# Moving the gate and up loads, and the work that needs them, in front of wq and K in a single-token decode kernel

## Chip, cores, metric

One core of one Trainium2 chip. The metric is the device time of one execution in microseconds (us), as a median of several. A kernel's executions mostly spread over 2 to 3 us. An execution counts as slow when it is over 1.5% above the fastest of the same kernel.

The engines go by short names: PE (TensorE, the matrix products; PEld its weight loads), DVE (VectorE), ACT (ScalarE), POOL (GpSimd) and SP (SyncE, which issues the loads; SPq is its queue of instructions). HBM is the memory that holds the inputs, SBUF the on-chip memory that the engines read. PE's granted clock is the share of its full clock that it was given.

## The reference

One token passes through attention over a long cache and through a feed-forward network, and a sigmoid gate mixes the two:

```python
# x: [1,1,512]; K, V: [1,32,65536,128]; wq: [512,4096]; wo: [4096,512]
# w_gate, w_up: [512,1792]; w_down: [1792,512]; all bf16
q = (x @ wq).reshape(32 heads, 128)
p = softmax(q . K * 128**-0.5)            # per head, over 65536 positions
a = (p @ V).reshape(4096) @ wo
b = (silu(x @ w_gate) * (x @ w_up)) @ w_down
g = sigmoid((x * gate_w).sum())
out = g * a + (1 - g) * b
```

K and V are 1073.7 MB together. Everything else is about 14 MB. Each byte is used once.

## The kernel before

SBUF holds a ring of three buffers ("slots") of 64 KB per partition. The work goes in 64 steps of 8.4 MB of K and 8.4 MB of V each (K0, V0, K1, V1, ...). A step multiplies K by q on DVE, in place, sums the products on PE against an identity, takes the exponential, and multiplies with V on PE ("P·V"). A load into a slot is issued on the SP queue and waits there until the slot's last reader has finished (K1's waited 47.0 us for the last gate/up product). In the first turn, wq, gate and up share the slot that K1 takes later:

```python
WQ = KT * H * Dh
wq_sb = view(0, 0, KT, H * Dh)
dma("wq", wq_sb, A_wq.rearrange("(p t) f -> p t f", t=KT), units(0, 0, WQ))
dma("x", x_row, A_x[0], ["x_row"], engine="ACT")
dma("gw", gw_row, gate_w.unsqueeze(0), ["gw_row"], engine="ACT")
# ... load(): each K or V step goes to the next of the three slots
load("k", 0, [EK] * (KPP // EK))          # four pieces of 64 rows per partition
G0, U0 = WQ, WQ + KT * F
gate_v, up_v = view(0, G0, KT, F), view(0, U0, KT, F)
dma("gate", gate_v, ...); dma("up", up_v, ...)
load("v", 0, [KPP])
# ... the q products: 128 matmuls of one column, reading wq
spread(0)
for n in range(N - 1):
    if n:
        load("k", n, [KPP]); load("v", n, [KPP])
    m = HK if n else EK
    for j in range(0, KPP, m):
        block(n, j, m)                    # K times q on DVE, sums on PE
        # ... elif n == N - 2: norm(0, H - 1); outputs()
        # ... gather(): reduce the sums on DVE, exp on ACT
    gather()
    if n == 0:
        gate()                            # the mixing gate
        hidden()                          # 112 gate/up matmuls, silu, product
    pv(n)
# the last step: w_down, wo, K63 in four pieces, V63 in five,
# with the down product and the attention output between the score blocks
```

The softmax here doesn't subtract the row's maximum and nothing guards it: scores larger than these inputs give would overflow.

## Time and profile before

| | before |
|---|---|
| time, median | 2522.44 us of 3 runs (2521.55 to 2523.16) |
| span of the profiled run | 2520.2 us |
| bytes moved, mean rate | 1088 MB, 432 GB/s |
| DMA, PE, DVE busy | 99.7%, 79%, 50% of the span |

These are lines of the page of the kernel before: span, busy time of each engine, the rate in 40 slices of 63 us, and the DMA queue that carries the loads.

```profile
span 2520.2 us, 19415 instructions
...
PE 1979.0 (79%) x9115; PEld 823.1 (33%) x9115; DVE 1268.4 (50%) x286; ACT 97.4 (4%) x398; POOL 1.9 (0%) x9
...
GB/s 423 430 432 433 435 433 434 434 435 436 435 435 434 433 434 435 434 434 434 435 436 434 435 433 434 434 435 435 434 433 435 436 435 435 433 433 434 436 429 359
...
q1 hardware_dynamic: 20880, 1087.78, 99.7%
```

The loads fill the span. Only the first slice (423) and the last two (429, 359) fall below the rate of the rest.

The windows view gives busy time per stretch; its last three columns are PE's granted clock, the DMA share and the rate. This is the kernel before, with its heading and two stretches of it:

```profile
core 0: us, PE busy (x) PEld busy (x) DVE busy (x) ACT busy (x) POOL busy (x), PEclk, DMA share, GB/s
...
55.00:60.00 5.00, 0.00 (x0) 0.00 (x0) 0.00 (x0) 0.00 (x0) 0.00 (x0) 0.50 1.03 446
...
80.00:2469.00 2389.00, 1888.81 (x8153) 772.70 (x8153) 1224.58 (x251) 90.04 (x369) 0.00 (x0) 0.91 1.00 434
```

In 2389 us in the middle the DMA share is 1.00 at 434 GB/s.

The third view is the DMA queue's own timeline in the opening (start, duration of the issue, what is loaded):

```profile
1.02 0.37 SPq L179 DMA_DIRECT2D slot_65<-in_A_wq_dram  x1
1.44 1.98 SPq L179 DMA_DIRECT2D slot_66<-in_A_k_cache_dram  x4
3.46 0.47 SPq L179 DMA_DIRECT2D slot_65<-in_B_w_gate_dram  x1
3.97 0.49 SPq L179 DMA_DIRECT2D slot_65<-in_B_w_up_dram  x1
4.50 0.45 SPq L179 DMA_DIRECT2D slot_67<-in_A_v_cache_dram  x1
51.96 0.33 SPq L179 DMA_DIRECT2D slot_65<-in_A_k_cache_dram  x1
52.33 0.43 SPq L179 DMA_DIRECT2D slot_66<-in_A_v_cache_dram  x1
77.94 0.33 SPq L179 DMA_DIRECT2D slot_67<-in_A_k_cache_dram  x1
```

The first eight loads are issued in the first 5 us and stand in the queue (V0 landed 57.4 us after its issue). K1 (slot_65) follows at 51.96 us, when the last gate/up product has ended. V1 (slot_66) stands behind it in the queue's order.

PE waited for two loads in the first 63 us. The first line is its wait for wq (us in total, times, longest); the second is P·V of step 0 from the timeline (start, duration, instruction, and in brackets how long PE was idle before it and what it waited for, here V0):

```profile
PE m_x L265 <- DMA slot_65<-in_A_wq_dram: 10.8, 1, 10.8
...
61.93 15.98 PE L251 MATMUL O_ps<-slot_67,P_sb_83 128*4 128x512 bf16 x64 [10.01 <-DMA slot_67<-in_A_v_cache_dram]
```

### The profile page before, as it was taken

Reading aid. Unit: us, or ns where it says so; the run is one execution under the profiler, and the core shown is the slowest. Engines: PE = TensorE matmul, PEld = TensorE weight load, DVE = VectorE, ACT = ScalarE, POOL = GpSimd, SP = SyncE. Lnnn points to the kernel's source line nnn. Section 1 sums busy time; section 2 is a strip of 40 time slices with the busy share of each in tenths; the row PEclk is TensorE's granted clock in tenths of the full one; section 3 lists DMA queues with packets and bytes.
Section 4 is the critical chain, followed back from the end, with each engine's and each line's share of the span. In section 5 each row is a group of like instructions: output and inputs, shape, how many; then the busy total and the mean of one; then the engine's idle time right before and its main releaser. Section 6 shows DMA issues by size and latency. Waiting matters only on the chain.

```text
span 2520.2 us, 19415 instructions
## 1 busy us (share of the span) xinstructions
PE 1979.0 (79%) x9115; PEld 823.1 (33%) x9115; DVE 1268.4 (50%) x286; ACT 97.4 (4%) x398; POOL 1.9 (0%) x9
## 2 busy tenths in 40 slices
PE   4787877877778778778787787787787877877878
PEld 2233332333333333333333333333333332333334
DVE  3455355464553554644645546446455455464553
ACT  0000000000000000000000000000000000000000
POOL 0000000000000000000000000000000000000000
PEclk8888988989889899899898898998998988989888
DMA  9999999999999999999999999999999999999998
GB/s 423 430 432 433 435 433 434 434 435 436 435 435 434 433 434 435 434 434 434 435 436 434 435 433 434 434 435 435 434 433 435 436 435 435 433 433 434 436 429 359
DMA packets 20906, 1088.09 MB, mean 432 GB/s; under 512 B 2450, under 2 KB 2580, under 8 KB 2836
## 3 DMA queue, kind: packets, MB, share of 16 engines
q1 hardware_dynamic: 20880, 1087.78, 99.7%
q8 instruction: 16, 0.26, 0.0%
q14 instruction: 6, 0.05, 0.0%
q10 hardware_dynamic: 4, 0.00, 0.0%
HBM read 1087.77 MB, written 0.00 MB: 432 GB/s over the span
## 4 chain that ended last, share of the span: by engine, by line
DMA 44%; PE 41%; DVE 13%; ACT 1%; another core or an unknown queue 0%; issue 0%; SPq 0%; DVEq 0%; ACTq 0%
PE O_ps L251 18%; DMA slot_67<-in_A_k_cache_dram 16%; DMA slot_66<-in_A_k_cache_dram 14%; DMA slot_65<-in_A_k_cache_dram 14%; PE S_ps_101 L265 12%; PE S_ps_102 L265 9%; DVE slot_66 L324 4%; DVE slot_67 L324 4%; DVE slot_65 L324 3%; DVE S_sb_82 L349 2%; PE m_c L251 2%; PE m_x L265 1%; ACT P_sb_83 L274 1%; DMA slot_65<-in_A_wq_dram 0%
## 5 line engine op out<-in xcount | busy, mean ns | idle before, releaser
L265 PE MATMUL S_ps_101<-slot_67,ident 128*128 128x512 bf16 x704 | 204.1, 462 | 134.5 <-DVE slot_67 L324 134.5
L265 PE MATMUL S_ps_101<-slot_66,ident 128*128 128x512 bf16 x672 | 196.6, 464 | 128.3 <-DVE slot_66 L324 128.3
L265 PE MATMUL S_ps_101<-slot_65,ident 128*128 128x512 bf16 x672 | 189.6, 452 | 132.6 <-DVE slot_65 L324 132.6
L324 DVE TENSOR_TENSOR slot_67<-slot_67,q_bc_79 128x16384 bf16<-128x16384 bf16 (+1 forms) x26 | 207.9, 8033 | 142.0 <-DMA slot_67<-in_A_k_cache_dram 142.0
L349 DVE TENSOR_REDUCE S_sb_82<-S_ps_102 128x128 f32<-128x1024 f32 (+1 forms) x66 | 78.7, 1192 | 387.9 <-PE S_ps_102 L265 387.9
L324 DVE TENSOR_TENSOR slot_65<-slot_65,q_bc_78 128x16384 bf16<-128x16384 bf16 x22 | 190.2, 8689 | 145.7 <-DMA slot_65<-in_A_k_cache_dram 145.7
L324 DVE TENSOR_TENSOR slot_66<-slot_66,q_bc_78 128x16384 bf16<-128x16384 bf16 (+1 forms) x24 | 190.6, 7977 | 136.1 <-DMA slot_66<-in_A_k_cache_dram 120.4
L324 DVE TENSOR_TENSOR slot_67<-slot_67,q_bc_78 128x16384 bf16<-128x16384 bf16 x20 | 172.9, 8689 | 121.9 <-DMA slot_67<-in_A_k_cache_dram 121.9
L324 DVE TENSOR_TENSOR slot_66<-slot_66,q_bc_79 128x16384 bf16<-128x16384 bf16 x20 | 172.9, 8688 | 118.7 <-DMA slot_66<-in_A_k_cache_dram 118.7
L324 DVE TENSOR_TENSOR slot_65<-slot_65,q_bc_79 128x16384 bf16<-128x16384 bf16 x20 | 172.9, 8689 | 118.5 <-DMA slot_65<-in_A_k_cache_dram 118.5
L251 PE MATMUL O_ps<-slot_67,P_sb_83 128*4 128x512 bf16 x704 | 155.7, 382 | 28.3 <-ACT P_sb_83 L274 18.3
L251 PE MATMUL O_ps<-slot_65,P_sb_83 128*4 128x512 bf16 x704 | 155.2, 381 | 20.7 <-ACT P_sb_83 L274 20.7
L251 PE MATMUL O_ps<-slot_66,P_sb_84 128*4 128x512 bf16 x704 | 153.7, 379 | 19.3 <-ACT P_sb_84 L274 19.3
L265 PEld LDWEIGHTS S_ps_101<-slot_67,ident 128*128 128x128 bf16 x704 | 79.1, 115 | 258.9 <-DVE slot_67 L324 145.1
L265 PEld LDWEIGHTS S_ps_101<-slot_66,ident 128*128 128x128 bf16 x672 | 75.7, 116 | 249.1 <-DVE slot_66 L324 139.0
L265 PE MATMUL S_ps_102<-slot_67,ident 128*128 128x512 bf16 x704 | 155.9, 379 | 0.2 <-DVE slot_67 L324 0.2
L265 PEld LDWEIGHTS S_ps_101<-slot_65,ident 128*128 128x128 bf16 x672 | 74.1, 113 | 248.4 <-DVE slot_65 L324 143.2
L251 PE MATMUL O_ps<-slot_65,P_sb_84 128*4 128x512 bf16 x640 | 139.7, 379 | 18.3 <-ACT P_sb_84 L274 18.3
L251 PE MATMUL O_ps<-slot_67,P_sb_84 128*4 128x512 bf16 x640 | 139.7, 379 | 18.3 <-ACT P_sb_84 L274 18.3
L251 PE MATMUL O_ps<-slot_66,P_sb_83 128*4 128x512 bf16 x640 | 139.7, 379 | 17.5 <-ACT P_sb_83 L274 17.5
L265 PE MATMUL S_ps_102<-slot_66,ident 128*128 128x512 bf16 x672 | 148.7, 379 | 1.3 <-DVE slot_66 L324 1.3
L265 PE MATMUL S_ps_102<-slot_65,ident 128*128 128x512 bf16 x672 | 148.6, 379 | 0.1
(83 smaller groups left out, 860.1 us busy)
## 6 DMA issues: line engine op xcount, KB each, us to landing
slot_66<-in_A_k_cache_dram SPq DMA_DIRECT2D x4, 2048.0 KB, 24.7
slot_67<-in_A_k_cache_dram SPq DMA_DIRECT2D x4, 2048.0 KB, 23.9
slot_65<-in_A_wq_dram SPq DMA_DIRECT2D x1, 4096.0 KB, 12.3
slot_66<-in_A_wo_dram SPq DMA_DIRECT2D x1, 4096.0 KB, 30.7
slot_65<-in_A_v_cache_dram SPq DMA_DIRECT2D x1, 4096.0 KB, 17.6
slot_65<-in_A_v_cache_dram SPq DMA_DIRECT2D x1, 2048.0 KB, 22.1
slot_65<-in_B_w_gate_dram SPq DMA_DIRECT2D x1, 1792.0 KB, 34.9
slot_65<-in_B_w_up_dram SPq DMA_DIRECT2D x1, 1792.0 KB, 38.6
```

Of the source, the lines that this page charges most:

```text
L251: ins = nc.tensor.matmul(out_ap, lhsT=a, rhs=b, start=start and i == 0, stop=stop and i == len(pairs) - 1,)
L265: ins = nc.tensor.matmul(out_ap, lhsT=a, rhs=b, start=(i == 0), stop=(i == len(pairs) - 1))
L274: "ACT", key, lambda: nc.scalar.activation(out=out_ap, in_=in_ap, func=func, **kw),
L324: "products", lambda: nc.vector.tensor_tensor(out=w, in0=w, in1=q_rep, op=ALU.mult),
L349: lambda: nc.vector.tensor_reduce(out=S_sb[b][:, :m], in_=S_ps[r][:, :m, :], axis=AXIS.X, op=ALU.add),
```

## The change

Its intent is to put the gate/up products and the mixing gate into the time in which PE waits for wq, so that they no longer stand between the scores of step 0 and its P·V. For that gate and up are loaded first, then wq, then K0. No byte and no matmul is added or removed. The diff, complete:

```diff
--- before.py
+++ after.py
@@ -183,6 +183,10 @@
 
     WQ = KT * H * Dh
     wq_sb = view(0, 0, KT, H * Dh)
+    G0, U0 = WQ, WQ + KT * F
+    gate_v, up_v = view(0, G0, KT, F), view(0, U0, KT, F)
+    dma("gate", gate_v, B_w_gate.rearrange("(p t) f -> p t f", t=KT), units(0, G0, U0))
+    dma("up", up_v, B_w_up.rearrange("(p t) f -> p t f", t=KT), units(0, U0, U0 + KT * F))
     dma("wq", wq_sb, A_wq.rearrange("(p t) f -> p t f", t=KT), units(0, 0, WQ))
     dma("x", x_row, A_x[0], ["x_row"], engine="ACT")
     dma("gw", gw_row, gate_w.unsqueeze(0), ["gw_row"], engine="ACT")
@@ -214,10 +218,6 @@
         assert at == KPP
 
     load("k", 0, [EK] * (KPP // EK))
-    G0, U0 = WQ, WQ + KT * F
-    gate_v, up_v = view(0, G0, KT, F), view(0, U0, KT, F)
-    dma("gate", gate_v, B_w_gate.rearrange("(p t) f -> p t f", t=KT), units(0, G0, U0))
-    dma("up", up_v, B_w_up.rearrange("(p t) f -> p t f", t=KT), units(0, U0, U0 + KT * F))
     load("v", 0, [KPP])
 
 
@@ -288,20 +288,6 @@
         ["x_row", "ones_b"], ["m_x"],
     )
     dve("Xc", lambda: nc.vector.tensor_copy(out=Xc, in_=m_x[:, :KT]), ["m_x"], ["Xc"])
-
-
-    group(
-        "q_ps",
-        [
-            (
-                m_x[:, h : h + 1],
-                [(wq_sb[:, t, h * Dh : (h + 1) * Dh], Xc[:, t : t + 1]) for t in range(KT)],
-            )
-            for h in range(H)
-        ],
-        units(0, 0, WQ) + ["Xc"], ["m_x"],
-    )
-    act("qT", qT, m_x[:, :H], ACT.Copy, ["m_x"], ["qT"])
 
     def spread(h):
 
@@ -497,6 +483,21 @@
 
     V_END = [KPP // 2, KPP // 4, KPP // 8, KPP // 16, KPP // 16]
     cut = {}
+    gate()
+    hidden()
+
+    group(
+        "q_ps",
+        [
+            (
+                m_x[:, h : h + 1],
+                [(wq_sb[:, t, h * Dh : (h + 1) * Dh], Xc[:, t : t + 1]) for t in range(KT)],
+            )
+            for h in range(H)
+        ],
+        units(0, 0, WQ) + ["Xc"], ["m_x"],
+    )
+    act("qT", qT, m_x[:, :H], ACT.Copy, ["m_x"], ["qT"])
     spread(0)
     for n in range(N - 1):
         h, c = divmod(n, CH)
@@ -519,9 +520,6 @@
             while len(todo) > 1:
                 gather()
         gather()
-        if n == 0:
-            gate()
-            hidden()
         if n == N - 2:
             turn_outputs(0)
         pv(n)
```

## The prediction

> # Prediction
>
> **What bounds the kernel now.** The DMA engines. The page gives the hardware queue 99.7% of 16 engines' span and a mean of 432 GB/s; 1087.8 MB at the 434 GB/s of most slices is about 2506 us of a 2520 us span (an estimate from those numbers). PE is busy 79% (1979 us), DVE 50% (1268 us). [...]
>
> **The opening, where the change is.** In windows of 5 us, the DMA share is 0.63 in the first and 0.95 or more in every one to 100 us: the queue never runs dry. The DMA-queue timeline shows why: later loads are issued ahead of their turn. K of step 1 (into the buffer of wq, gate and up) is issued at 51.96 us, after the last gate/up product, while V of step 0 lands until 61.93 us (PE's wait for it ends there): 10 us to spare. V of step 1 is issued at 52.33 us, behind it.
>
> **What the change does.** No byte and no matmul is added or removed: the same loads go out in another order, and the 112 gate/up matmuls (6.85 us), the mixing gate (about 2 us) and six small ACT/DVE steps (about 1.4 us) move from after K0's scores to the wait for wq. PE idles there now: 10.8 us until 13.38 us.
>
> Estimates from this trace's rate and landings:
> - gate+up (3.67 MB) take 8.5 us and land near 12 us; their products end at 16 to 19 us; wq lands near 22 us instead of 13.4; the 128 q matmuls (3.58 us) end near 25.5 us.
> - DVE's first K product starts near 27 us instead of 18.46. The K pieces land every 4.8 us, the last near 41 us; scores are ready near 50 us instead of 44.
> - V0 lands at 62 us as before, since the same bytes precede it. P·V of step 0 starts there in both kernels: the 8.5 us lost on K are absorbed by PE's wait for V0 (10 us now, about 11 then, since gate/up no longer stand in it).
> - K1 is issued near 25.5 us instead of 52 and only sits in the queue longer; V1 near 49.5 us instead of 52.3, held by K0's last sums.
>
> **On the critical path: about 0 us.** From 62 us on both kernels should be in the same state, and the end is untouched (last DMA bytes at about 2511 us, then the last products and the output). What remains is noise of the tail: PE runs without a gap from 2469 to 2511 us, and its granted clock there (0.69 to 1.00 in windows) can move the end by a microsecond or two.
>
> **Predicted time:** 2522.4 us, range 2519.0 to 2526.0. Chances: faster by over 2% 0.005, within 2% 0.99, slower 0.005.
>
> **What would show it right.** DMA share near 1 from 5 us on; gate/up matmuls at 12 to 19 us, q matmuls at 22 us, first K product at 27 us; K1 issued at 25 us; P·V of step 0 starting within 1 us of 62 us; GB/s from the second slice on unchanged.
>
> **What would make it wrong.** If DMA really starved between 45 and 62 us, an earlier K1 would gain up to a few us. If the shorter runs per partition of gate and up (14 KB against 32 KB of wq) slow the first transfers, that costs directly. If K now paces the scores past 62 us, V1's issue slips, but it would have to slip past about 80 us to cost anything. Another phase of PE's clock in the last 50 us could move the time 1 to 2 us for no reason in the change.

The 2522.4 us are the time of the kernel before (2522.44 us) with about 0 us on the critical path.

## More of the kernel before

The gate/up matmuls read their weights at a step of 14 columns, so that hidden unit `p*14+ft` falls on partition p, as w_down is laid out:

```python
[(wv[:, t, bass.ds(ft, P, FT)], Xc[:, t : t + 1]) for t in range(KT)]
```

## The result, and the profile after

The changed kernel took 2521.99 us (median of 4 runs, 2521.67 to 2523.99), the kernel before 2522.29 us (4 runs). The ratio is 1.000, with a 95% interval of 0.9983 to 1.0018: the same time. A ratio here is the mean time of one kernel's fast runs over that of the other's of the same rounds, so it is not quite the ratio of the medians.

The same lines of the page of the changed kernel:

```profile
span 2520.0 us, 19416 instructions
...
PE 1979.7 (79%) x9115; PEld 823.9 (33%) x9115; DVE 1268.3 (50%) x286; ACT 97.4 (4%) x398; POOL 1.9 (0%) x9
...
q1 hardware_dynamic: 20880, 1087.78, 99.7%
```

The window of the middle (same columns as before):

```profile
80.00:2469.00 2389.00, 1889.01 (x8153) 773.23 (x8153) 1224.45 (x251) 90.06 (x368) 0.00 (x0) 0.91 1.00 434
```

Busy times, bytes and rate are unchanged.

The queue's timeline after the change:

```profile
1.03 0.37 SPq L179 DMA_DIRECT2D slot_65<-in_B_w_gate_dram  x1
1.45 0.43 SPq L179 DMA_DIRECT2D slot_65<-in_B_w_up_dram  x1
1.92 0.42 SPq L179 DMA_DIRECT2D slot_65<-in_A_wq_dram  x1
2.39 2.35 SPq L179 DMA_DIRECT2D slot_66<-in_A_k_cache_dram  x4
4.79 0.45 SPq L179 DMA_DIRECT2D slot_67<-in_A_v_cache_dram  x1
26.92 0.33 SPq L179 DMA_DIRECT2D slot_65<-in_A_k_cache_dram  x1
53.14 0.33 SPq L179 DMA_DIRECT2D slot_66<-in_A_v_cache_dram  x1
78.04 0.33 SPq L179 DMA_DIRECT2D slot_67<-in_A_k_cache_dram  x1
```

K1 is now issued at 26.92 us, 25 us earlier. V1 is issued at 53.14 us, K2 (slot_67) at 78.04 us against 77.94 us: the advance is gone when the ring has turned once, because K2 needs V0's slot, and V0 lands when it did before. PE's waits, and P·V of step 0, show the same thing:

```profile
PE m_x L265 <- DMA slot_65<-in_B_w_up_dram: 5.4, 1, 5.4
...
PE m_x L265 <- DMA slot_65<-in_A_wq_dram: 3.4, 1, 3.4
...
62.01 16.01 PE L251 MATMUL O_ps<-slot_67,P_sb_83 128*4 128x512 bf16 x64 [8.90 <-DMA slot_67<-in_A_v_cache_dram]
```

PE's wait for V0 ended at 61.93 us before and ends at 62.01 us now. The wait for wq went from 10.8 to 3.4 us, and a wait of 5.4 us for up was added. The work did move into the idle time as intended. The end of the idle time did not move, since the same bytes come before V0 in any order.

### The profile page after: what moved, and what is told of

Same layout as the page of the kernel before. It is cut to its first block, busy times and chain, and to the rows that moved or that the text cites. A ratio compares the mean times of both kernels' runs of the same rounds, so it can differ in the third digit from the quotient of the medians.

```text
span 2520.0 us, 19416 instructions
## 1 busy us (share of the span) xinstructions
PE 1979.7 (79%) x9115; PEld 823.9 (33%) x9115; DVE 1268.3 (50%) x286; ACT 97.4 (4%) x398; POOL 1.9 (0%) x9
## 3 DMA queue, kind: packets, MB, share of 16 engines
q1 hardware_dynamic: 20880, 1087.78, 99.7%
## 4 chain that ended last, share of the span: by engine, by line
DMA 45%; PE 41%; DVE 13%; ACT 1%; issue 0%; another core or an unknown queue 0%; SPq 0%; DVEq 0%; ACTq 0%
PE O_ps L251 18%; DMA slot_67<-in_A_k_cache_dram 16%; DMA slot_66<-in_A_k_cache_dram 14%; DMA slot_65<-in_A_k_cache_dram 14%; PE S_ps_101 L265 12%; PE S_ps_102 L265 9%; DVE slot_66 L310 4%; DVE slot_67 L310 4%; DVE slot_65 L310 3%; DVE S_sb_82 L335 2%; PE m_c L251 2%; DMA slot_65<-in_A_wq_dram 1%; ACT P_sb_83 L274 1%; PE m_x L265 0%
## 5 line engine op out<-in xcount | busy, mean ns | idle before, releaser
L251 PE MATMUL O_ps<-slot_66,P_sb_84 128*4 128x512 bf16 x704 | 153.7, 379 | 19.3 <-ACT P_sb_84 L274 19.3
```

The lines of the kernel that those rows point to most:

```text
L251: ins = nc.tensor.matmul(out_ap, lhsT=a, rhs=b, start=start and i == 0, stop=stop and i == len(pairs) - 1,)
```

## Experiments

The theory to be tested (Q): the DMA queue sets the time; what PE and DVE do in the opening costs nothing as long as the next load is issued before the queue runs dry. The rival (C): the opening's work is on the critical path, and the change made two real shifts that cancel, about 9 us gained by clearing the way from scores to P·V and about 9 us lost by loading K0 later. Both fit a ratio of 1.000. Twelve kernels were run. They were timed in batches. Each batch ran on one chip, with runs of the kernel before among them, and a kernel is compared only with those of its own batch (the factors 2 and 6 below were in another batch, on another chip, than the factor 4).

Medians against the kernel before of the same rounds ("K62 ready" is the start of DVE's first product on the K of step 62 in the profiled run, 2439.53 us in the kernel before):

| run | this, us (runs) | before, us (runs) | ratio, 95% interval | K62 ready, us |
|---|---|---|---|---|
| loads_only | 2526.41 (5) | 2522.78 (9) | 1.0013, 1.0000 to 1.0027 | 2442.64 |
| pe_only | 2523.78 (5) | 2522.78 (9) | 1.0004, 0.9990 to 1.0017 | 2441.56 |
| before_gu2 | 2523.57 (5) | 2522.98 (9) | 1.0001, 0.9987 to 1.0015 | 2440.52 |
| before_gu4 | 2535.54 (4) | 2522.78 (9) | 1.0050, 1.0034 to 1.0065 | 2451.98 |
| after_gu4 | 2524.25 (4) | 2522.78 (9) | 1.0005, 0.9990 to 1.0020 | 2440.01 |
| after_gu6 | 2527.00 (4) | 2522.98 (9) | 1.0017, 1.0002 to 1.0032 | 2444.21 |
| no_up | 2518.07 (5) | 2522.98 (9) | 0.9981, 0.9967 to 0.9994 | 2435.24 |
| down_early | 2525.21 (5) | 2522.98 (9) | 1.0010, 0.9996 to 1.0023 | 2443.98 |
| tail_pieces | 2522.43 (5) | 2522.41 (9) | 0.9999, 0.9985 to 1.0012 | in pieces |
| tail_pieces_down | 2522.28 (5) | 2522.41 (9) | 1.0000, 0.9986 to 1.0013 | in pieces |
| tail_pieces_before | 2521.29 (5) | 2522.41 (9) | 0.9997, 0.9984 to 1.0011 | in pieces |
| gu_contig | 2522.03 (1, state unknown) | 2524.17 (1, state unknown) | none | |

The intervals are about 0.0013 (3 us) wide on each side. Where a time differs by less, the trace's own instants are what is read.

Not every time fell into the range expected. Those of before_gu4, after_gu6 and no_up did. Those of pe_only, before_gu2 and after_gu4 lie up to 0.6 us above the range that Q gave, and that of loads_only 1.4 us; down_early and the three tail_pieces kernels missed theirs too. Each of these was slower than expected, none faster.

### The two halves of the change, each alone

loads_only takes the new order of loads and leaves PE's order as it was:

```diff
 wq_sb = view(0, 0, KT, H * Dh)
+dma("gate", ...); dma("up", ...)
 dma("wq", ...)
 ...
 load("k", 0, ...)
-dma("gate", ...); dma("up", ...)
```

> The new load order with the old order on PE (gate/up products after the scores of K0). Theory Q (the DMA queue sets the time; work in the opening is free as long as the next load is issued before the queue runs dry): K0's scores end near 54 us as in the changed kernel, the gate/up products run from about 55 to 62 us, so K1 is issued at about 62 us, at the very moment when V0's last bytes land: the queue runs dry for 1 to 2 us and the time is 2523 to 2525 us. Rival C (the opening's work is on the critical path; the change gains about 9 us by clearing the work between K0's scores and P*V of step 0, and loses about 9 us by loading K0 later): this half has the loss alone, so about 2531 us.

Measured: 3.6 us slower (2526.41 against 2522.78 us; no run of the one overlaps the other's).

```profile
60.91 0.33 SPq L179 DMA_DIRECT2D slot<-in_A_k_cache_dram  x1
...
84.22 17.29 DVE L324 TENSOR_TENSOR slot<-slot,q_bc 128x16384 bf16<-128x16384 bf16 x2 [21.96 <-DMA slot<-in_A_k_cache_dram]
```

K1 was issued at 60.91 us, and the first product on K1 started at 84.22 us, 3.0 us later than the 81.20 us of the kernel before. K62 was ready 3.1 us late. That is more than the dry time of 1 to 2 us expected, although K1 was issued a little earlier than foreseen (the margin was mis-sized, see the points below), and far less than the 9 us of C.

pe_only does the reverse: PE's new order (gate/up, then q), and the loads in the old order. Its edit is against the changed kernel:

```diff
-dma("gate", ...); dma("up", ...)        # in front of wq
 dma("wq", ...)
 ...
 load("k", 0, ...)
+dma("gate", ...); dma("up", ...)
```

> The old load order with the new order on PE (gate/up products before the q products, so q waits for up, which lands last). Q: gate/up products 42.6 to 49.5 us, q until 53 us, K1 issued near 53 us (before V0 has landed at 62 us), first K product near 54.5 us instead of 18.5, K0's scores near 80 us, P*V of step 0 at 80 us instead of 62, V1 issued near 79 us, just before K1's bytes end at about 81: time 2522 to 2523.5 us although the first step is 18 us late. C: 15 to 20 us slower, about 2540 us.

These are lines of its timeline (start, duration, instruction):

```profile
54.99 8.76 DVE L310 TENSOR_TENSOR slot<-slot,q_bc 128x8192 bf16<-128x8192 bf16 x2 [5.46 <-ACT q_bc L274]
...
79.25 0.33 SPq L179 DMA_DIRECT2D slot<-in_A_v_cache_dram  x1
...
80.38 13.97 PE L251 MATMUL O_ps<-slot,P_sb 128*4 128x512 bf16 x64 [1.16 <-ACT P_sb L274]
```

DVE's first product comes at 54.99 us instead of 18.46 us, and P·V of step 0 begins at 80.38 us, 18 us late. The time is 2523.78 us, 1.0 us above the kernel before and inside the noise of the timing. C's 15 to 20 us are not there. What is there is small and visible in the trace: K62 was ready 2.0 us late. K1, issued at 53.52 us, was in time (its first product at 81.16 us, against 81.20 us in the kernel before). V1, issued at 79.25 us, was not, so by Q it found the queue run dry. The window from 79 to 80 us shows no bytes (0 GB/s), but one empty microsecond proves little: the kernel before has one too, from 58 to 59 us, with K1 long in its queue.

So neither half gives the gain or the loss that C needs; C falls.

### How much slack there was: gate/up products made two, four or six times

The edit is one factor, in either kernel; the result stays right, since each pass overwrites the last:

```diff
-group("gu", parts, ...)
+group("gu", parts * 4, ...)             # 2, 4 or 6
```

> The kernel before with the gate/up products made twice. Q: K1 is issued at 51.96 + 6.85 = 58.8 us, 2 to 3 us before V0's bytes end: within the margin, so 2522 to 2523 us. Rival C: plus 6.85 us, 2529 us.

> The kernel before with the gate/up products made four times (three extra groups of 6.85 us, same result). Q: K1 is issued at 51.96 + 20.6 = 72.5 us, V0's bytes end near 61.5 us, so the queue is dry for some 12 us that are never recovered: about 2534 us (2532 to 2536). C predicts the full 20.6 us: about 2543 us. If neither the queue nor the opening matters: 2522 us.

Measured: twice costs 0.6 us in the median (ratio 1.0001, inside the noise); K1 was issued at 58.15 us and its first product started at 82.17 us, 1.0 us late. Four times costs 12.8 us, which is less than the 19.6 us that K1's issue moved, and about what Q gave. Here is DVE's first product on K1 in the kernel before (its issue, at 51.96 us, was shown above):

```profile
81.20 8.69 DVE L324 TENSOR_TENSOR slot_65<-slot_65,q_bc_78 128x16384 bf16<-128x16384 bf16 x1 [27.90 <-DMA slot_65<-in_A_k_cache_dram]
```

and both in before_gu4:

```profile
71.58 0.33 SPq L179 DMA_DIRECT2D slot<-in_A_k_cache_dram  x1
...
93.44 8.69 DVE L324 TENSOR_TENSOR slot<-slot,q_bc 128x16384 bf16<-128x16384 bf16 x1 [20.52 <-DMA slot<-in_A_k_cache_dram]
```

with before_gu4's window from 60 to 71 us:

```profile
60.00:71.00 11.00, 11.00 (x187) 11.00 (x186) 0.00 (x0) 0.00 (x0) 0.00 (x0) 0.50 0.01 3
```

The DMA share is 0.01 for 11 us, while PE works without a pause. K1's first product is 12.24 us late, K62 is 12.45 us late, and the time is 12.8 us longer: the time in which the queue was dry was not recovered by the end of the run.

> The changed kernel with the gate/up products made four times. Q: K1 is issued at 26.9 + 20.6 = 47.5 us (K0 and V0 still on their way), V1 at 53.1 + 20.6 = 73.7 us (K1's bytes run until about 81 us): no dry queue, 2522 us (2521 to 2524). C: wq's wait hides 3 us of it, the rest is paid: about 2539 us.

> The changed kernel with the gate/up products made six times (34 us extra). Q: K1 is issued at 26.9 + 34.3 = 61.2 us, on the edge; but V1, which waits for the last sums of K0, is issued at 53.1 + 34.3 = 87.4 us, and K1's bytes end near 81 to 82 us: the queue is dry for 5 to 7 us there and 0 to 1 us before, so about 2529 us (2527 to 2531). The changed kernel's margin would thus be set by V1, near 27 us, not by K1's 35 us. If only K1's issue mattered: 2522 to 2524 us. C: about 2553 us.

The changed kernel takes the same fourfold work for 1.5 us in the median (ratio 1.0005, interval with 1.0 in it). K62 was ready at 2440.01 us, 0.5 us later than in the kernel before. The rest arose in the tail, on PE: P·V of step 62 took 16.88 us in that trace, against 15.43 us in the kernel before, at a granted clock of 0.50 from 2470 to 2474 us (0.70 in the kernel before). Sixfold costs 4.0 us. From 80 to 84 us no bytes arrive; this is one half of that (after_gu6, window):

```profile
82.00:84.00 2.00, 1.15 (x6) 0.30 (x4) 0.81 (x2) 0.09 (x1) 0.00 (x0) 1.00 0.00 0
```

V1 was issued at 83.18 us, when K1's bytes had been over since about 80 us (147 GB/s from 79 to 80 us, 0 in each microsecond from there to 84 us); K1, issued at 57.53 us, still came in time. So in the changed kernel V1 is the first to be late, as expected.

This is what the change does: it raises the slack of the opening. In the kernel before 6 us more on PE already begin to show; after the change 17 us are free within the noise (K1's issue at 43.64 us instead of 26.92, V1's at 69.75 us instead of 53.14, in after_gu4). The kernel does not use that slack, so the time is the same.

### Fewer bytes

no_up loads no up weights and uses gate twice. Its output is wrong, which doesn't matter for the time.

```diff
-dma("up", up_v, ...)
-for w, wv in enumerate((gate_v, up_v)):
+for w, wv in enumerate((gate_v, gate_v)):
```

> The kernel before without the load of up (gate stands in for it, wrong result on purpose): 1.835 MB fewer, all engine work the same. Q: 1.835 MB at 434 GB/s is 4.2 us, so about 2518.1 us (2517.3 to 2519). If engine work and not bytes set the time: 2522 us.

Measured: 2518.07 us, 4.9 us faster in the median; K62 was ready 4.29 us earlier. These are DVE's first product on K62 in the kernel before and in no_up:

```profile
2439.53 17.30 DVE L324 TENSOR_TENSOR slot_67<-slot_67,q_bc_79 128x16384 bf16<-128x16384 bf16 x2 [12.33 <-DMA slot_67<-in_A_k_cache_dram]
...
2435.24 17.29 DVE L323 TENSOR_TENSOR slot<-slot,q_bc 128x16384 bf16<-128x16384 bf16 x2 [12.19 <-DMA slot<-in_A_k_cache_dram]
```

The estimate from 1.835 MB at the 434 GB/s of the trace was 4.2 us. The same engine work with fewer bytes was faster; more engine work in the opening with the same bytes cost nothing that the timing shows (0.6 us in before_gu2, 1.5 us in after_gu4), until the queue ran dry (12.8 us in before_gu4).

### Using the slack: the down product in the opening

down_early builds on the changed kernel. It loads w_down third, into the slot that V0 takes afterwards, and makes the down product while wq is loading. V0's load waits for it and is issued at 23.35 us.

```diff
 dma("gate", ...); dma("up", ...)
+dma("wd", wd, ..., units(2, 0, WO))
 dma("wq", ...)
 ...
 gate(); hidden()
+rows("b_ps", wd, ..., hT, "hT", range(FT)); dve("rest", ...)
+load("v", 0, [KPP])
 ...
-dma("wd", ...)                           # in the tail
-rows("b_ps", ...); dve("rest", ...)      # in the tail
```

> The changed kernel, going one step further: w_down is loaded third, into the buffer that V0 takes later, and the down product and its scaling (56 matmuls, 1.84 us in the tail of the trace) are made while wq loads; the tail loads and computes them no more. Same bytes. If the last 40 us are set by PE (it runs without a gap from 2469 us to the end, and the last bytes come near 2511 to 2512 us while PE still has 3 us of products): 1 to 2 us faster, 2520 to 2521 us. If the last bytes alone set the end: 2522 us. Everything between is shifted by the 4.2 us that w_down takes in front.

Measured: 2525.21 us, 2.2 us slower (the ratio's interval just includes 1.0, but all five runs lie above all nine of the kernel before). Neither expectation held. The tail explains it. In the chain of waits (start, duration, what), the changed kernel has:

```profile
2439.49 8.70 DVE slot_67 L310
...
2448.24 8.96 PE S_ps_101 L265 x32
...
2469.48 15.47 PE O_ps L251 x64
...
2485.15 3.56 PE S_ps_101 L265 x16
...
2491.52 3.56 PE S_ps_102 L265 x16
```

and down_early:

```profile
2443.98 8.70 DVE slot L313
...
2452.73 9.67 PE S_ps L268 x32
...
2474.70 15.66 PE O_ps L254 x64
```

From the moment when K62 has landed, DVE and PE follow one another nearly without a gap to the end: 8.70 us of products, the sums, P·V of step 62, then the last step. K62 became ready 4.49 us later than in the changed kernel, since w_down's 1.8 MB (4.2 us) now stand in front of it instead of behind it. The 56 matmuls taken out of the tail give 1.84 us back. The sum is 2.6 us; 2.2 were measured in the medians, 3.1 between the two profiled runs. So what the queue sets is the landing of K62. Loads after it (w_down, wo, K63, V63) come to their end at about the same time as PE, but PE is the later one: in the windows of the kernel before hardly any bytes arrive after 2512 us (0, 16 and 0 GB/s in the three microseconds to 2515 us), while PE has products until 2515 us.

That was a new theory (P), made after the run, so it was tested. tail_pieces loads and scores K62 in four pieces, as step 63 already is, so that the chain can start earlier. tail_pieces_down adds that to down_early, tail_pieces_before to the kernel before.

```diff
-load("k", n, [KPP])
+load("k", n, [KPP] if n < N - 2 else [EK] * (KPP // EK))
-m = HK if n else EK
+m = HK if 0 < n < N - 2 else EK
-elif n == N - 2:
+elif n == N - 2 and j == KPP // 2:
     norm(0, H - 1); outputs()
```

> The changed kernel with K of the last but one step loaded in four pieces of 64 rows per partition and scored piece by piece, as the last step already is. Same bytes. Theory P (the end is a chain on DVE and PE that starts when the whole K62 has landed at 2439.5 us, and PE finishes about 3 us after the last bytes; so bytes and dry time before K62's landing cost their full time, bytes behind it do not): DVE starts about 14 us earlier, the scores of step 62 end near 2458 us in place of 2467, P*V of step 62 starts near 2460 us in place of 2469, PE gets ahead of the loads and only the products of the last pieces follow the last bytes: 2 to 3 us faster, 2519.5 to 2520.5 us. Rival D (the last bytes set the end): 2522 us, no change.

> The kernel with w_down's load and the down product in the opening (2525.2 us, slower than expected by 3 to 4 us), with the same pieces for K62. P: its loss came from w_down's 1.8 MB (4.2 us) moving from behind K62's landing to in front of it, less the 1.84 us of products; with PE no longer last the place of the bytes does not matter and it is about as fast as the run above, 2519.5 to 2520.5 us, 5 us faster than without the pieces. Rival E (the early load of w_down itself slows the loads or leaves the queue dry): it stays 3 us slower than the run above, about 2523 us.

> The kernel before, with the pieces for K62 alone: shows whether the order of the opening is worth anything once the end follows the last bytes. P: the same 2519.5 to 2520.5 us as with the changed opening. If the changed order were worth something that the tail hides: 1 us or more slower than the run with the changed opening.

Measured: 2522.43, 2522.28 and 2521.29 us, with ratios of 0.9999, 1.0000 and 0.9997. All three times are 0.8 to 1.9 us above the 2519.5 to 2520.5 us foreseen. The first of these expectations missed: the pieces bring no 2 to 3 us, so P's account of the last 40 us is not complete. The second held in what told the theories apart: the 2.2 us that down_early had lost are gone, so it was the place of w_down's bytes relative to K62 and not a fault of its early load. The third held in that comparison too: with the pieces, the old and the new opening lie within the noise of each other (their runs overlap, 2521.14 to 2523.89 and 2521.25 to 2523.83 us).

Where the expected 2 to 3 us went can be followed in the chain of tail_pieces:

```profile
2478.45 4.44 DVE slot L310
...
2482.93 3.63 PE S_ps L265 x16
...
2489.47 5.09 PE S_ps L265 x16
...
2512.89 0.84 issue
```

P·V of step 62 did start earlier (2467.58 us against 2469.48 us in the changed kernel). But then PE had to wait for the first piece of K63, which DVE received at 2478.45 us, so the sums of step 63 began at 2482.93 us instead of 2485.15 us. Of those 2.2 us, 1.5 were lost at once: the second group of sums took 5.09 us against 3.56 us, with a granted clock of 0.68 from 2490 to 2494 us where the changed kernel had 1.00. PE's wait before the first sums, 1.18 us, had ended some 7 us before the lower clock came. In the changed kernel the clock also fell while PE was busy without a pause (0.73 from 2498 to 2502 us, at the end of 128 products of one column each). So the cause of the lower clock stays open. Another 0.84 us is a pause in the last products that the profile puts down to nothing ("issue"); whether it was the wait for a late piece of V63 stays open. PE's last product ended at 2516.16 us here and at 2515.69 us in the changed kernel: nothing was left of the 1.9 us by which P·V of step 62 started earlier.

No version with a right result beat the two kernels clear of the noise.

### Why one gate/up product takes twice as long as one q product

In the traces 112 gate/up products took 6.85 us and 128 q products 3.58 us, both with 128x128 weights and one column. gu_contig reads neighbouring columns instead of every 14th. Its hidden units are then in the wrong order for w_down, so its result is wrong.

```diff
-wv[:, t, bass.ds(ft, P, FT)]
+wv[:, t, ft * P : (ft + 1) * P]
```

> The changed kernel with the gate/up weights read as 128 neighbouring columns in place of every 14th (28 bytes apart); the hidden units then stand in another order than w_down's rows, so the result is wrong on purpose. If the step between the columns is why one gate/up product takes 61 ns (6.86 us for 112, at granted clocks of both 0.54 and 1.00) and one q product 28 ns: 112 products take 3.1 to 3.2 us. If something else in this place slows them: 6.8 us. In both cases 2522 us, since this work is not what the time waits for.

PE's timeline in the changed kernel, where the group of 112 is gate/up and the one of 128 is q:

```profile
13.03 6.86 PE L265 MATMUL m_x<-Xc,slot_65 128*128 128x1 bf16 x112 [5.42 <-DMA slot_65<-in_B_w_up_dram]
23.31 3.57 PE L265 MATMUL m_x<-Xc,slot_65 128*128 128x1 bf16 x128 [3.43 <-DMA slot_65<-in_A_wq_dram]
```

and in gu_contig:

```profile
12.75 3.13 PE L265 MATMUL m_x<-Xc,slot 128*128 128x1 bf16 x112 [5.18 <-DMA slot<-in_B_w_up_dram]
```

From 6.86 to 3.13 us, or from 61 to 28 ns each: the step between the columns was the whole difference. The clock was not: in the kernel before the same products took 6.85 us at a granted clock of 0.54, in the changed kernel 6.86 us at 1.00. Why the step of 14 costs this is not shown: no run here tries another step at this place. The attention output's products, at a step of 4, took 4.24 us for 128 in the chain of waits of the changed kernel, 33 ns each, at a granted clock of 1.00 from 2494 to 2498 us; that is more than the 28 ns at step 1, but no run here isolates the cause. The one look gave 2522.03 us for gu_contig and 2524.17 us for the kernel before beside it; single runs do not tell that difference from the spread of 2 to 3 us, and the profiled span of gu_contig was 2520.2 us, as in the kernel before.

## Why the prediction was right, point by point

- **The limit.** Right. The DMA queue sets the time up to the landing of K62: 4.2 us of bytes taken away gave 4.3 us there (no_up), and 11 us of a dry queue cost 12.8 us (before_gu4).
- **Nothing of the change on the critical path.** Right. P·V of step 0 starts at 62.01 us against 61.93 us, K2 is issued at 78.04 us against 77.94 us, and the time is the same. The risk named in the prediction, that the shorter runs of gate and up slow the first transfers, would have shown in the first two of these, which moved by 0.08 and 0.10 us. That the median came within 0.4 us of the forecast is less than the spread of the runs and proves nothing by itself. That it is not a gain and a loss that cancel is shown by the two halves, which cost 3.6 and 1.0 us and not 9 or more.
- **The moves within the opening.** Near: gate/up products at 13.0 to 19.9 us (foreseen 12 to 19), q products from 23.31 us (22), first K product at 28.39 us (27), K1 issued at 26.92 us (25.5).
- **K0's scores near 50 us, V1 near 49.5 us.** Off by 4 us: V1 was issued at 53.14 us. The prediction let the four pieces be paced by their landing every 4.8 us. In the trace they had landed in time; DVE paced them, with 4.42 us of product and 0.69 us of reduction for each piece, and the first group of sums took 6.56 us, during which the reduction and all DVE work queued behind it waited (2.13 us). The wait for V0 absorbed this as well: it was 8.9 us long, not the 11 foreseen.
- **"10 us to spare" for K1.** Mis-sized. The prediction took the end of PE's wait for V0 as the moment when the queue runs dry. The last bytes are over earlier, at about 60 us (in before_gu4, whose queue held nothing behind V0, 131 GB/s from 59 to 60 us, 16 in the next microsecond, then none), and the load issued after them did not bring bytes at once (K1, issued there at 71.58 us, shows none until 72 us and 918 GB/s from 72 to 73 us; from its issue to the first product on it were 21.9 us, of which 8.4 MB at 434 GB/s are 19.3, so that about 2.5 us are left over, an estimate from these numbers). An issue at 58.15 us delayed K1 by 1.0 us, at 60.91 us by 3.0 us, at 71.58 us by 12.2 us: the limit lies (by subtracting each delay) near 57 to 59 us, 3 to 5 us before PE's wait for V0 ended at 61.93 us, so 5 to 7 us were to spare. In the opening neither kernel issued a load past its limit, so the mistake did not reach the forecast. The same holds for V1: "past about 80 us" should have been 77 to 79 us (an issue at 79.25 us delayed K62 by 2.0 us, at 83.18 us by 4.7 us). In the changed kernel V1 is thus the nearest to its limit, with 24 to 26 us to spare.
- **The tail.** "Another phase of PE's clock" is seen: after_gu4 lost 1.45 us in P·V of step 62 at a lower clock (0.50 from 2470 to 2474 us, against 0.70 in the kernel before). The prediction saw the last bytes at about 2511 us and PE without a gap before them, but not where this begins; down_early showed a chain on DVE and PE from K62's landing. This touched nothing in the change itself.

## What to carry to other kernels

Here the load queue was busy for 99.7% of the span, and moving engine work into an idle stretch bought slack (K1 issued 25 us earlier), not time (ratio 1.000). So look for the instant at which each later load is issued and compare it with the instant at which the bytes ahead of it end, not with the consumer's wait for them: the bytes of V0 were over at about 60 us in before_gu4, while PE's wait for V0 ended at 61.93 us in the kernel before. Every issue was early enough in both kernels, and the change was worth nothing; adding work on purpose measured how much slack there was (K1 issued 17 us later stayed within the noise after the change, while 19.6 us later cost the kernel before 12.8 us). Near the end the order of bytes did matter: w_down (1.8 MB), moved from behind K62 to in front of it, delayed K62 and the chain of work that hangs on it by 4.49 us.
